# A hand-written order planned anew: transfers taken to land later, one quad more in the second chunk, other limits for the fillers

## The chip, the cores and the metric

The kernel runs on one core of a Trainium2 chip. The metric is device time in microseconds of one execution; several runs are made, and their median counts. One execution was also recorded by the hardware profiler; its span runs from the first to the last instruction of the program.

## What is computed

One transformer block with conditioning: a modulation vector from `c`, layer norm, attention with 32 heads of 20, a residual, a second layer norm, and a gated product of two projections, with a second residual. There are 2048 rows of 640, and 1536 hidden columns; all arrays are bf16.

```python
def _A_ref(x, wqkv, wo):
    qkv = (x @ wqkv).reshape(B, S, 3, H, Dh).transpose(2, 0, 3, 1, 4)
    q, k, v = qkv[0], qkv[1], qkv[2]
    scores = jnp.einsum('bhqd,bhkd->bhqk', q, k) * Dh ** (-0.5)
    p = _softmax(scores, axis=-1)
    o = jnp.einsum('bhqk,bhkd->bhqd', p, v)
    return o.transpose(0, 2, 1, 3).reshape(B, S, D) @ wo
def _B_ref(x, w_gate, w_up, w_down):
    h = jnp.einsum('bsd,df->bsf', x, w_gate) * jnp.einsum('bsd,df->bsf', x, w_up)
    return jnp.einsum('bsf,fd->bsd', h, w_down)
mod = (_silu(c) @ w_mod).reshape(c.shape[0], 6, 1, -1)
sa, ca, ga, sb, cb, gb = (mod[:, i] for i in range(6))
h = _layernorm(x) * (1 + ca) + sa
x = x + ga * _A_ref(h, A_wqkv, A_wo)
h = _layernorm(x) * (1 + cb) + sb
x = x + gb * _B_ref(h, B_w_gate, B_w_up, B_w_down)
```

## The kernel before

**A planner writes the order.** Nothing in this program is ordered by hand. While the program is built, `Sched` plays through all of the work with assumed durations, picks for each engine what to issue next, and `emit_program` then writes the five engines' instruction streams in exactly that order, with semaphore waits where one engine needs another's result. On the chip each engine keeps its order: where a result is later than the planner assumed, the engine waits, with all that stands behind. The assumed durations thus set the order and nothing else.

**Chunks, items, units.** The 2048 query rows are cut into seven chunks (`CHUNKS`: one of 512, six of 256). A chunk is worked through in eight items, each of four heads. An item's scores are cut into units: one head, and as many key tiles of 128 as fill 512 columns of a PSUM bank (four for a chunk of 512 rows, two for one of 256). The four heads of an item lie in four row groups of TensorE, so units of different heads run side by side (L1525).

**Two ways to exponentiate.** Most units go in pairs to ScalarE: one ACTIVATE of 128 x 1024 reads two banks and writes the ring `PP` (L1562). `QUADS` says how many quads (four units each) of each item of a chunk go to VectorE instead. For those VectorE adds a bias and rounds to int16 (L1586, one instruction a unit, into `DB`), masks the mantissa (L1618) and the exponent (L1626) of the whole quad into `DSS`, and a product completes the first of two terms: either one instruction on VectorE (L1623) or four pieces on GpSimd (L1638), whichever the planner finds free. The products with V (L2193) take one term from `PP`, but two from `DSS`.

**What TensorE interleaves.** Between two stretches of scores TensorE works on products with V, and on one round after another of other work: at the start layer norm transposes (L1128), the projections to K, Q (L1167, L1231) and V (L971 with wV), later the second half of the block for the chunk before ("suffix": output projection with `wo`, transposes, gate and up products with weights in `stg`, down products with `wd`). K and Q of most heads are laid out anew through DRAM: copied to `KPA` or `KPB`, written to `k_rows` or `q_rows` (L1277), and read back into `KT` (L1290) and `QT` (L1299). Finished attention goes through `OT`, `OTn`, `OcT` and then by DMA to `Ocp` (L1747). The weights in `stg` come through three buffers (L1932). All of these transfers stand in one queue, SyncE's, in the planner's order.

**What the planner assumes of transfers.** `Sched.finish_issue` (in the print below) sets `task.done`, the time at which a DMA is taken to have landed: issue, size over a rate, a latency, and for those issued after `DMA_M0` (60 us) a margin, `DMA_MARGIN`.

**Fillers.** The planner also models the clock of TensorE from the activity in windows of `HAM_W` ns (`roll`, with `HAM_MIN` as the least activity of a window that counts as busy). `do_fill` issues four matmuls that change no result, or a product that adds zero (`zero_fill`, L2524), where recent activity is below `FILL_HARD` or, for other picks, `FILL_MIN`; a full-width filler stands at L2552, one of four column groups at L2554.

**Stage settings.** `STAGE` maps an item's number (0 to 56, eight per chunk) to settings that hold from that item on: how many products with V are gathered before a switch (`PVMIN`, `PVMAX`, `PVCAP`), how long TensorE holds back for scores that are about to be ready (`HOLD`, `PVTOL`), when VectorE's units are pulled forward (`EAGER`, `D_LATE`, `D_RES`, `DL`), when a round's matmul is cut in two halves (`X_LATE`, `X_HALF`), and the limits above.

Of the kernel before, what the change touches and what calls it, by code (L numbers as in the profile page):

```python
# [26 lines left out]
DMA_SLOW = 0.0015  # L27
DMA_LAT = 1700.0
DMA_RATE_2 = 240.0
DMA_MARGIN = 500.0  # L30
DMA_M0 = 60000.0
STEAL_END = 66197.894
STEAL_GAP = 200
HAM_W = 3413.3
HAM_MIN = 3000.0
LKTOL = 300.0


# [92 lines left out]
class Sched:  # L131
# [78 lines left out]
    def roll(self, t):  # L210
        for i in range(4):
            w = int((t - i * HAM_W / 4) // HAM_W)
            while self.ham_w[i] < w:
                low = self.ham_act[i] < HAM_MIN
                if low:
# [18 lines left out]
    def finish_issue(self, task, start, dur):  # L234
        task.start = start
        if task.nbytes:
            early = self.t < DMA_EARLY
            b = max(self.dma_free, start + dur + (DMA_LAT_1 if early else 0.0))
            self.dma_free = b + task.nbytes / (DMA_RATE if early or task.firm else DMA_RATE_2)
            task.done = task.land or self.dma_free + (DMA_LAT_2 if early else DMA_LAT + DMA_SLOW * task.nbytes +  # L240
                                                      (0.0 if task.firm or start < DMA_M0 else DMA_MARGIN))
        else:
            task.done = start + dur + task.lat
        self.order[task.eng].append(task)
        self.all.append(task)
        self.left -= 1
        if task.on_start is not None:
            task.on_start(task)
        for u in task.users:
            u.nleft -= 1  # L250
            if u.nleft == 0:
                self._enable(u)
        task.users = []
# [99 lines left out]
def emit_program(nc, sched, nsem_dma=56):  # L353
# [121 lines left out]


CHUNKS = ((0, 512), (512, 256), (768, 256), (1024, 256), (1280, 256), (1536, 256), (1792, 256))
QUADS = ((0, 4, 3, 3, 3, 4, 4, 4), (1, 2, 1, 2, 2, 2, 1, 2), (2, 2, 1, 2, 2, 2, 1, 2), (2, 2, 1, 2, 2, 2, 1, 2), (2, 2, 1, 2, 2, 2, 1, 2), (2, 2, 1, 2, 2, 2, 1, 2), (2, 1, 2, 2, 2, 1, 2, 0))
SPLITJ = 1
QHALF = ((0, 0), (0, 0))  # L480
TB_GATE = 2
# [2 lines left out]
PV_KEEP = 2  # L484
# [10 lines left out]
EAGER = 7  # L495
# [3 lines left out]
XBACK = 0  # L499
HOLD = 110  # L500
PVTOL = 249
XDPRIO = 1.343
TPRIO = 0.75
# [19 lines left out]
D_LATE = 16  # L523
D_RES = 20
PVMIN, PVMAX, PVCAP = 2, 7, 12
# [13 lines left out]
GATE_F = (0.446, 0.5, 0.5, 0.5, 0.5, 0.5, 1.0)  # L539
FILL_MIN = 4190.746  # L540
HARD_FROM = 16000
FILL_HARD = 3500.0
FILL_T0, FILL_TH, FILL_MINH = 2300.0, 17000.0, 7500.0
FILL_MODE = 'P'
DUP_MIN = 0.0
# [17 lines left out]
NTERM = 2  # L563

STAGE = {
    0: {"XBACK": 0, "PVMAX": 14, "TPRIO": 0.75, "D_LATE": 16, "STEAL_GAP": 200, "EAGER": 9, "PVTOL": 249, "HOLD": 68.4, "PV_KEEP": 2, "X_HALF": 0.0, "XDPRIO": 1.343, "PVMIN": 2, "D_RES": 74, "LKTOL": 300.0, "X_LATE": -179.96, "FILL_MIN": 4190.746, "PVCAP": 12},
    2: {"DL": 0.376},
    4: {"PV_KEEP": 4, "XBACK": 1},
    5: {"EAGER": 5},
    6: {"STEAL_GAP": 303.6, "FILL_MIN": 4369.6},  # L570
    7: {"DL": 0.501, "EAGER": 12, "LKTOL": 214.2, "HOLD": 125.5},
    10: {"PVMAX": 5, "EAGER": 9, "FILL_MIN": 4030.1},
    11: {"DL": 0.443, "HOLD": 147.1, "PVCAP": 10, "EAGER": 1, "PVMAX": 13},
    12: {"DL": 0.459, "X_HALF": -78.2},
    13: {"DL": 0.417},
    14: {"X_HALF": 0.1, "D_RES": 9, "PVTOL": 152.2, "PVCAP": 7, "X_LATE": 15.9},
    15: {"PVTOL": 269.4, "X_LATE": 118.5},
    16: {"D_RES": 72, "HOLD": 109.5},
    17: {"XBACK": 1},
    18: {"HOLD": 26.4, "D_RES": 21, "PV_KEEP": 1, "FILL_MIN": 4542.4},  # L580
    19: {"DL": 0.471, "D_RES": 8, "EAGER": 5},
    20: {"DL": 0.391},
    21: {"EAGER": 9, "FILL_MIN": 4229.0, "PV_KEEP": 2},
    22: {"HOLD": 191.0},
    23: {"HOLD": 87.8, "PVMAX": 5},
    24: {"DL": 0.464, "STEAL_GAP": 189.1, "X_LATE": -52.5, "PVCAP": 14},
    25: {"DL": 0.549, "EAGER": 2, "PVMIN": 2, "PVMAX": 3, "STEAL_GAP": 204.7},
    26: {"DL": 0.411, "EAGER": 2, "PVMIN": 2, "PVCAP": 14},
    27: {"DL": 0.473, "X_LATE": -44.8},
    28: {"FILL_MIN": 4986.9},  # L590
    29: {"PVTOL": 317.6, "PVMAX": 4},
    30: {"EAGER": 11, "LKTOL": 263.3, "X_LATE": -102.4},
    31: {"FILL_MIN": 4003.8, "XBACK": 1, "PV_KEEP": 1},
    32: {"HOLD": 173.2, "X_HALF": 164.9, "PV_KEEP": 2},
    33: {"DL": 0.442, "PV_KEEP": 3, "LKTOL": 517.2},
    35: {"X_HALF": -49.0},
    36: {"DL": 0.524, "LKTOL": 130.0, "X_LATE": -54.5, "XBACK": 1},
    37: {"PVMAX": 9, "D_RES": 9, "X_LATE": 42.7, "D_LATE": 12},
    39: {"EAGER": 6, "X_LATE": -3.0, "XBACK": 2},
    40: {"FILL_MIN": 4681.4, "HOLD": 77.9},  # L600
    43: {"X_HALF": -36.2, "D_LATE": 18, "HOLD": 133.6, "STEAL_GAP": 190.9, "PV_KEEP": 2},
    44: {"PV_KEEP": 2, "X_HALF": -31.7},
    48: {"XBACK": 1},
    51: {"X_HALF": 18.4},
    56: {"D_RES": 25, "FILL_MIN": 4778.8},
}
XHALF = 1
STG_G0, STG_G, XC_G = 12, -10, -20
X_LATE = -24.052
X_HALF = 0.0  # L610
# [10 lines left out]
def build_kernel(nc, A_x, A_wqkv, A_wo, B_x, B_w_gate, B_w_up, B_w_down, c, w_mod, out):  # L621
# [710 lines left out]
    spans = [(0, CHUNKS[ci][1]) for ci, _ in items]  # L1332
    nqs = [QUADS[ci][j] for ci, j in items]
    if SPLITJ:
# [934 lines left out]
    def half_x(t):  # L2269
        cand = xcur[0]  # L2270
        if not XHALF or cand is None or id(cand) not in halves or ring() < RINGLOW:
            return False
        if any(d.done is None or d.done + SEM > t for d in cand.deps):
            return False
        sr = s_ready()
        if sr is None or t >= sr:
            return False
        start = mode_start(cand.mode, t)
        late = start + cand.dur - sr - X_LATE
        if late <= 0 or late - cand.dur / 2 > X_HALF:  # L2280
            return False
        first, cand.emits = halves.pop(id(cand))
        cand.dur /= 2
        h = Task("pe", cand.dur, first, cand.deps, ctr="pex", mode=cand.mode, name=cand.name, prio=cand.prio)
        h.seq = 0
        sc.left += 1
        sc.activity(start, h.dur * 2.37)
        sc.finish_issue(h, start, h.dur * clk())
        sc.pe_mode = h.mode
        sc.pe_end = start + h.dur * clk()  # L2290
        sc.free_at["pe"] = sc.pe_end
        nhalf[0] += 1
        return True
# [103 lines left out]
    def pick_pe(t):  # L2397
# [65 lines left out]
        if HOLD and sr is not None and t < sr <= t + HOLD and ring() >= RINGLOW:  # L2463
            return half_x(t)
        if sc.recent(t) < FILL_HARD and t > HARD_FROM and do_fill(t):
            return True
# [163 lines left out]
```

## Time and profile before

| what | value |
|---|---|
| runs | 810.54, 810.21, 807.32 us; median 810.21 |
| profiled execution: run time | 808.72 us |
| profiled execution: span | 806.9 us |
| mean granted TensorE clock | 0.998 |
| busy: PE / DVE / ACT / POOL | 790.6 / 691.5 / 765.1 / 395.4 us |
| instructions | 37691 |
| DMA | 64.65 MB, mean 80 GB/s |

How to read it: a matmul's end is modelled, and matmuls of different row or column groups overlap, so the busy time of PE says that it always had work in flight, not that it ran at its peak. Durations in a group are means of one instruction from start to end; where such instructions overlap in the pipeline, the step from one start to the next is shorter than the mean. Views that list instructions in order of time give the start in us from the beginning of the span, the length of the merged group, the engine, the line, what is written and read, the count, and in brackets how long the engine was idle before it and what ended that wait. Line numbers are those of the kernel before; in the changed kernel most lines stand one line earlier.

### The profile page before, as it was taken

Reading aid. Unit: us, or ns where it says so; the run is one execution under the profiler, and the core shown is the slowest. Engines: PE = TensorE matmul, PEld = TensorE weight load, DVE = VectorE, ACT = ScalarE, POOL = GpSimd, SP = SyncE. Lnnn points to the kernel's source line nnn. Section 1 sums busy time; section 2 is a strip of 40 time slices with the busy share of each in tenths; the row PEclk is TensorE's granted clock in tenths of the full one; section 3 lists DMA queues with packets and bytes.
Section 4 is the critical chain, followed back from the end, with each engine's and each line's share of the span. In section 5 each row is a group of like instructions: output and inputs, shape, how many; then the busy total and the mean of one; then the engine's idle time right before and its main releaser. Section 6 shows DMA issues by size and latency. Waiting matters only on the chain.

```text
span 806.9 us, 37691 instructions
## 1 busy us (share of the span) xinstructions
PE 790.6 (98%) x16551; PEld 377.7 (47%) x16551; DVE 691.5 (86%) x1392; ACT 765.1 (95%) x848; POOL 395.4 (49%) x408
## 2 busy tenths in 40 slices
PE   8999999999999999999999999999999999999998
PEld 3433433332244344444555555545554555455567
DVE  6979788889989999998798988999899989799654
ACT  6799899999999999999999999999999999999961
POOL 2345455556464564554636555543554455554300
PEclk9999999999999999999999999999999999999999
DMA  9743312212342441120052224312420244414420
GB/s 293 214 137 81 77 36 70 71 33 65 89 110 56 141 112 45 40 55 21 23 123 53 57 57 104 73 29 66 113 65 15 63 106 87 104 39 89 107 66 18
DMA packets 154313, 64.65 MB, mean 80 GB/s; under 512 B 116951, under 2 KB 154151, under 8 KB 154151
## 3 DMA queue, kind: packets, MB, share of 16 engines
q1 hardware_dynamic: 153223, 61.10, 29.8%
q8 instruction: 131, 2.15, 1.1%
q10 hardware_dynamic: 928, 1.15, 0.4%
q14 instruction: 31, 0.25, 0.1%
HBM read 50.63 MB, written 8.99 MB: 74 GB/s over the span
## 4 chain that ended last, share of the span: by engine, by line
PE 67%; ACT 20%; DVE 5%; issue 4%; DMA 3%; SPq 1%; POOL 0%; ACTq 0%; DVEq 0%
PE ps_all L1525 23%; ACT PP L1562 20%; PE ps_all L971 19%; PE ps_all L2193 16%; PE ps_all L1231 3%; PE ps_all L967 3%; DMA x<-in_A_x_dram 2%; DVE DB L1586 2%; DMA stg<-in_B_w_up_dram 1%; PE ps_all L1890 1%; DVE DSS L1618 1%; PE ps_all L1128 0%; DVE DSS L1626 0%; SPq L1747 0%; PE ps_all L2524 0%
## 5 line engine op out<-in xcount | busy, mean ns | idle before, releaser
L1562 ACT ACTIVATE PP<-ps_all 128x1024 bf16<-128x1024 f32 x812 | 749.5, 1108 | 8.0 <-PE ps_all L1525 4.0
L1638 POOL TENSOR_TENSOR DSS<-DB,DSS 128x512 bf16<-128x512 bf16 x280 | 317.3, 1155 | 290.7 <-DVE DSS L1626 255.1
L1586 DVE TENSOR_SCALAR DB<-ps_all 128x512 int16<-128x512 f32 x424 | 285.1, 683 | 49.8 <-PE ps_all L1525 46.4
L1525 PE MATMUL ps_all<-QT,KT 32*128 32x256 bf16 (+2 forms) x3648 | 319.9, 287 | 6.4 <-ACT PP L1562 2.5
L1525 PEld LDWEIGHTS ps_all<-QT,KT 32*128 32x128 bf16 x3648 | 93.2, 92 | 207.8 <-ACT PP L1562 149.3
L2193 PE MATMUL ps_all<-PP,Vf 128*32 128x256 bf16 (+2 forms) x2900 | 165.5, 291 | 0.8 <-DVE Vf L1320 0.7
L971 PE MATMUL ps_all<-h2T,stg 128*32 128x256 bf16 (+2 forms) x2728 | 124.8, 280 | 0.8 <-DMA stg<-in_B_w_up_dram 0.3
L2193 PEld LDWEIGHTS ps_all<-PP,Vf 128*32 128x32 bf16 (+1 forms) x2900 | 53.5, 94 | 79.3 <-issue 70.9
L2193 PE MATMUL ps_all<-DSS,Vf 128*32 128x256 bf16 (+1 forms) x1496 | 86.2, 290 | 0.0
L971 PEld LDWEIGHTS ps_all<-h2T,stg 128*32 128x32 bf16 x2728 | 61.8, 96 | 28.1 <-issue 21.0
L1626 DVE TENSOR_SCALAR DSS<-DB 128x2048 int16<-128x2048 int16 x106 | 74.0, 698 | 0.8 <-PE ps_all L2193 0.8
L1618 DVE TENSOR_SCALAR DSS<-DB 128x2048 int16<-128x2048 int16 x106 | 73.4, 693 | 0.5
L971 PE MATMUL ps_all<-wd,hprod 128*32 128x320 bf16 (+1 forms) x1364 | 62.4, 280 | 0.0
L1726 POOL TENSOR_TENSOR OTn<-OT,invT 128x256 bf16<-128x256 f32 (+1 forms) x49 | 34.6, 707 | 35.0 <-DVE invT L1724 34.9
L1623 DVE TENSOR_TENSOR DSS<-DB,DSS 128x2048 bf16<-128x2048 bf16 x36 | 44.9, 1248 | 0.1
L2193 PEld LDWEIGHTS ps_all<-DSS,Vf 128*32 128x32 bf16 x1496 | 34.5, 95 | 21.7 <-issue 14.6
L971 PE MATMUL ps_all<-wV,hT 128*32 128x160 bf16 x1280 | 38.7, 234 | 0.4 <-DVE DB L1586 0.2
L971 PEld LDWEIGHTS ps_all<-wd,hprod 128*32 128x32 bf16 x1364 | 30.9, 96 | 14.2 <-issue 11.2
L1718 DVE STREAM_TRANSPOSE OT<-ps_all 128x256 f32<-128x256 f32 (+2 forms) x57 | 27.1, 475 | 7.3 <-PE ps_all L2193 7.1
L1231 PE MATMUL ps_all<-hT,wk 128*32 128x512 bf16 (+1 forms) x360 | 32.8, 386 | 0.0
L971 PEld LDWEIGHTS ps_all<-wV,hT 128*32 128x32 bf16 x1280 | 24.4, 96 | 15.4 <-issue 8.2
L1231 PE MATMUL ps_all<-hT,wq 128*32 128x512 bf16 x375 | 31.5, 382 | 0.0
(133 smaller groups left out, 557.7 us busy)
## 6 DMA issues: line engine op xcount, KB each, us to landing
stg<-in_B_w_gate_dram SPq DMA_DIRECT2D x74, 160.0 KB
stg<-in_B_w_up_dram SPq DMA_DIRECT2D x74, 160.0 KB
KT<-k_rows SPq DMA_DIRECT2D x112, 32.0 KB
QT<-q_rows SPq DMA_DIRECT2D x48, 64.0 KB
Ocp<-OcT SPq DMA_DIRECT2D x164, 10.0 KB
wm<-in_w_mod_dram SPq DMA_DIRECT2D x3, 800.0 KB
x<-in_A_x_dram SPq DMA_DIRECT2D x7, 320.0 KB
k_rows<-KPA SPq DMA_DIRECT2D x16, 128.0 KB
```

What stands on the lines that cost most here:

```text
L971: return lambda e, b: e.matmul(ps[32 * x:32 * x + 32, b, c0 + o:c0 + o + w], lhs()[:, 32 * x:32 * x + 32], rhs() if w == n else rhs()[:, o ...
L1231: f = [lambda e, b_, k=k, x=x: e.matmul(ps[x:x + min(32, w - x), b_, :], wx[:, k, r0 + x:r0 + min(x + 32, w)], hT[tc][:, k, :], tile_posit ...
L1525: ems.append(lambda e, i=i, kt=kt: e.matmul(dstf()[:, i * u.n:(i + 1) * u.n], KT[32 * u.s:32 * u.s + 32, u.j, kt * 128:(kt + 1) * 128], QT ...
L1562: return e.activation(PPs[g % 2][:, cellp["p"], 0:nu * 512], ps[:, b0:b0 + nu, :].rearrange("p b c -> p (b c)"), AFT.Exp, scale=ESCALE)
L1586: return e.tensor_scalar(DBl[st_["slot"]][:, x * 512:(x + 1) * 512], bank(cell["b"]), EBIAS, 0.0, op0=ALU.add, op1=ALU.max)
L1618: return e.tensor_scalar(DSl[st_["ss"][0]][:, :], DBl[st_["slot"]][:, :], 0x7F, 0x3F00, op0=ALU.bitwise_and, op1=ALU.bitwise_or)
L1623: return e.tensor_tensor(d, DBl[st_["slot"]][:, :].bitcast(BF16), d, ALU.mult)
L1626: return e.tensor_scalar(DSl[st_["ss"][1]][:, :], DBl[st_["slot"]][:, :], 0x7F80, 2, op0=ALU.bitwise_and, op1=ALU.bitwise_or)
L1638: return e.tensor_tensor(d, DBl[st_["slot"]][:, x * w:x * w + w].bitcast(BF16), d, ALU.mult)
L1718: t1 = Task("dve", n * 1.1 + 70, lambda e: e.transpose(OT[:, 0:n], ps[:, item_info[it]["bank"], 0:n].rearrange("p (b q r) -> p b r q", q=3 ...
L1726: f3 = lambda e: e.tensor_tensor(OTn[:, 0:n].rearrange("p (b c r) -> p b r c", c=32, r=2), OT[:, 0:n].rearrange("p (b r c) -> p b r c", c= ...
L2193: ems.append(lambda e, i=i, kt=kt, stt=stt, stp=stp: e.matmul(ps[32 * s:32 * s + mc, bk, 0:u.n], Vf[:, (kt * H + 4 * u.j + s) * VW:(kt * H ...
```

## The change

The assumed landing of transfers is put later: `DMA_MARGIN` from 500 to 1000 ns for those issued after 60 us, and a new `EARLY_M` of 900 ns for those in the first 25 us whose priority number is 0.9 or more (the first half of the V weights, the third and fourth 512 rows of x, the second halves of the weights). `HAM_MIN` goes from 3000 to 3100 and `FILL_HARD` from 3500 to 3600. The first item of chunk 1 has two quads instead of one. `STAGE` is replaced in most of its entries. Since every one of these goes into the planner, the order of all five engines is another from the first microseconds on.

```diff
-DMA_MARGIN = 500.0
+DMA_MARGIN = 1000.0
+EARLY_M = 900.0
...
-HAM_MIN = 3000.0
+HAM_MIN = 3100.0
...
+            if early and not task.land and task.prio >= 0.9:
+                task.done += EARLY_M
...
-QUADS = ((0, 4, 3, 3, 3, 4, 4, 4), (1, 2, 1, 2, 2, 2, 1, 2), ...
+QUADS = ((0, 4, 3, 3, 3, 4, 4, 4), (2, 2, 1, 2, 2, 2, 1, 2), ...
...
-FILL_HARD = 3500.0
+FILL_HARD = 3600.0
...
 STAGE = {
-    0: {"XBACK": 0, "PVMAX": 14, "TPRIO": 0.75, "D_LATE": 16, "STEAL_GAP": 200, "EAGER": 9, "PVTOL": 249, "HOLD": 68.4, "PV_KEEP": 2, "X_HALF": 0.0, "XDPRIO": 1.343, "PVMIN": 2, "D_RES": 74, "LKTOL": 300.0, "X_LATE": -179.96, "FILL_MIN": 4190.746, "PVCAP": 12},
+    0: {"PVMIN": 2, "HOLD": 95, "PVTOL": 249, "D_RES": 58, "PVCAP": 6, "X_HALF": 0.0, "XDPRIO": 1.343, "FILL_MIN": 3463.3, "LKTOL": 300.0, "EAGER": 9, "PVMAX": 14, "X_LATE": -179.96, "TPRIO": 0.75, "STEAL_GAP": 200, "D_LATE": 16, "PV_KEEP": 2},
+    1: {"PVCAP": 15, "XBACK": 1, "FILL_MIN": 4629.7},
     2: {"DL": 0.376},
-    4: {"PV_KEEP": 4, "XBACK": 1},
-    5: {"EAGER": 5},
-    6: {"STEAL_GAP": 303.6, "FILL_MIN": 4369.6},
-    7: {"DL": 0.501, "EAGER": 12, "LKTOL": 214.2, "HOLD": 125.5},
+    4: {"HOLD": 58.0, "X_LATE": -39.3},
+    5: {"D_LATE": 7, "PVMAX": 3},
+    6: {"X_LATE": 168.4, "FILL_MIN": 5225.9, "HOLD": 156.4},
+    7: {"DL": 0.501},
...
```

What the two orders hold, counted: exponentials of ScalarE 812 and 810; first steps of VectorE 424 and 428; products on VectorE 36 and 40; pieces on GpSimd 280 and 268; matmuls 16,551 and 16,595; DMAs of SyncE the same. The stretches of scores on TensorE are 833 and 826.

More of the change, by code (lines that the diff above doesn't have):

```diff
@@ L477 @@
 CHUNKS = ((0, 512), (512, 256), (768, 256), (1024, 256), (1280, 256), (1536, 256), (1792, 256))
-QUADS = ((0, 4, 3, 3, 3, 4, 4, 4), (1, 2, 1, 2, 2, 2, 1, 2), (2, 2, 1, 2, 2, 2, 1, 2), (2, 2, 1, 2, 2, 2, 1, 2), (2, 2, 1, 2, 2, 2, 1, 2), (2, 2, 1, 2, 2, 2, 1, 2), (2, 1, 2, 2, 2, 1, 2, 0))
+QUADS = ((0, 4, 3, 3, 3, 4, 4, 4), (2, 2, 1, 2, 2, 2, 1, 2), (2, 2, 1, 2, 2, 2, 1, 2), (2, 2, 1, 2, 2, 2, 1, 2), (2, 2, 1, 2, 2, 2, 1, 2), (2, 2, 1, 2, 2, 2, 1, 2), (2, 1, 2, 2, 2, 1, 2, 0))
 SPLITJ = 1
@@ L567 @@
+    1: {"PVCAP": 15, "XBACK": 1, "FILL_MIN": 4629.7},
     2: {"DL": 0.376},
-    4: {"PV_KEEP": 4, "XBACK": 1},
-    5: {"EAGER": 5},
-    6: {"STEAL_GAP": 303.6, "FILL_MIN": 4369.6},
-    7: {"DL": 0.501, "EAGER": 12, "LKTOL": 214.2, "HOLD": 125.5},
-    10: {"PVMAX": 5, "EAGER": 9, "FILL_MIN": 4030.1},
-    11: {"DL": 0.443, "HOLD": 147.1, "PVCAP": 10, "EAGER": 1, "PVMAX": 13},
-    12: {"DL": 0.459, "X_HALF": -78.2},
-    13: {"DL": 0.417},
-    14: {"X_HALF": 0.1, "D_RES": 9, "PVTOL": 152.2, "PVCAP": 7, "X_LATE": 15.9},
@@ L577 @@
[L577 to L605, printed above, removed]
+    4: {"HOLD": 58.0, "X_LATE": -39.3},
+    5: {"D_LATE": 7, "PVMAX": 3},
+    6: {"X_LATE": 168.4, "FILL_MIN": 5225.9, "HOLD": 156.4},
+    7: {"DL": 0.501},
+    8: {"FILL_MIN": 2868.8},
@@ new lines @@
+    10: {"X_HALF": 69.3, "HOLD": 73.7, "PVMAX": 5},
+    11: {"DL": 0.443},
+    12: {"DL": 0.459, "HOLD": 108.3, "X_LATE": 6.6},
+    13: {"DL": 0.417},
+    15: {"X_LATE": 86.8},
+    16: {"HOLD": 135.0, "FILL_MIN": 4362.5},
+    17: {"X_LATE": -17.4, "LKTOL": 338.9, "HOLD": 52.0},
+    19: {"DL": 0.471, "PVMAX": 7, "HOLD": 113.6},
+    20: {"DL": 0.391, "PVMAX": 10},
+    21: {"X_LATE": -85.4, "PVMIN": 3},
+    24: {"DL": 0.464, "STEAL_GAP": 210.6, "X_LATE": -52.5, "PVCAP": 14, "HOLD": 116.4, "LKTOL": 98.1},
@@ new lines @@
+    25: {"DL": 0.549, "LKTOL": 370.4, "HOLD": 156.3},
+    26: {"DL": 0.411, "PVMIN": 1, "X_LATE": 2.0, "EAGER": 6, "X_HALF": 58.0},
+    27: {"DL": 0.473},
+    29: {"HOLD": 148.6, "D_LATE": 5, "LKTOL": 267.5, "D_RES": 36, "PVMAX": 3},
+    30: {"EAGER": 11},
+    31: {"X_LATE": -99.6, "HOLD": 173.2, "X_HALF": 164.9, "PV_KEEP": 2},
+    33: {"DL": 0.442, "PVMIN": 7, "PV_KEEP": 3, "X_HALF": 147.4},
+    34: {"PVMIN": 3, "X_HALF": 26.9, "STEAL_GAP": 91.8, "EAGER": 8, "X_LATE": 136.8, "D_RES": 25},
@@ L606 @@
+    35: {"X_HALF": 148.7},
+    36: {"DL": 0.524},
+    37: {"FILL_MIN": 4112.0, "EAGER": 8, "X_LATE": -201.5},
+    39: {"STEAL_GAP": 162.9, "EAGER": 9},
+    42: {"PVMAX": 8, "FILL_MIN": 4334.4, "PV_KEEP": 3},
+    43: {"HOLD": 127.6},
+    46: {"D_LATE": 20, "PV_KEEP": 3, "X_LATE": -80.9},
+    53: {"LKTOL": 820.1, "X_HALF": 73.5},
+    54: {"PVTOL": 279.6, "FILL_MIN": 4011.5, "X_HALF": 31.3},
 }
```

## The prediction

> **What bounds the kernel now.** I read the profiled execution: span 806.9 us, run time 808.72 us, so 1.8 us lie around the span; the median of the three runs (810.21) is 1.5 us above this run. First the chain that ended last and the costliest groups:
>
> ```profile
> PE 67%; ACT 20%; DVE 5%; issue 4%; DMA 3%; SPq 1%; POOL 0%; ACTq 0%; DVEq 0%
> ...
> L1562 ACT ACTIVATE PP<-ps_all 128x1024 bf16<-128x1024 f32 x812 | 749.5, 1108 | 8.0 <-PE ps_all L1525 4.0
> L1638 POOL TENSOR_TENSOR DSS<-DB,DSS 128x512 bf16<-128x512 bf16 x280 | 317.3, 1155 | 290.7 <-DVE DSS L1626 255.1
> L1586 DVE TENSOR_SCALAR DB<-ps_all 128x512 int16<-128x512 f32 x424 | 285.1, 683 | 49.8 <-PE ps_all L1525 46.4
> ...
> L1626 DVE TENSOR_SCALAR DSS<-DB 128x2048 int16<-128x2048 int16 x106 | 74.0, 698 | 0.8 <-PE ps_all L2193 0.8
> L1618 DVE TENSOR_SCALAR DSS<-DB 128x2048 int16<-128x2048 int16 x106 | 73.4, 693 | 0.5
> ...
> L1623 DVE TENSOR_TENSOR DSS<-DB,DSS 128x2048 bf16<-128x2048 bf16 x36 | 44.9, 1248 | 0.1
> ```
>
> Two engines share the bound: TensorE has most of the chain, but ScalarE's 812 exponentials form one almost unbroken stream. Second, ScalarE in order of time (start, length, count, idle before):
>
> ```profile
> 16.35 4.66 ACT L1562 ACTIVATE PP<-ps_all 128x1024 bf16<-128x1024 f32 x5
> ...
> 92.92 1.94 ACT L1562 ACTIVATE PP<-ps_all 128x1024 bf16<-128x1024 f32 x2 [2.77 <-PE ps_all L2193]
> ...
> 149.54 66.30 ACT L1562 ACTIVATE PP<-ps_all 128x1024 bf16<-128x1024 f32 x72
> ...
> 753.02 25.79 ACT L1562 ACTIVATE PP<-ps_all 128x1024 bf16<-128x1024 f32 x28 [0.58 <-PE ps_all L1525]
> ```
>
> The 72 exponentials from 149.54 come every (66.30 - 1.02)/71 = 0.92 us (1.02 is the length of a single one), although the group's mean length is 1.108: they overlap. So 0.92 is the price of one. The stream runs from 16.35 to 753.02 + 25.79 = 778.81; 812 x 0.92 = 747 of these 762.5 us is its own pace, some 15 us are stalls, and 28.1 us of tail follow. The time is start + count x pace + stalls + tail, and the change is costed in these terms.
>
> Third, the start, by stage (PE, weight loads, DVE, ACT, POOL busy, then granted clock):
>
> ```profile
> 17.50:20.00 2.50, 1.78 (x23) 0.51 (x18) 2.50 (x10) 2.50 (x4) 1.06 (x2) 1.00 0.70 179
> 20.00:22.50 2.50, 1.94 (x20) 0.97 (x20) 2.50 (x8) 1.91 (x3) 1.39 (x3) 0.89 1.11 332
> 22.50:25.00 2.50, 2.50 (x20) 1.17 (x22) 2.23 (x7) 1.83 (x3) 0.37 (x2) 0.50 0.31 65
> 25.00:27.50 2.50, 2.50 (x61) 1.32 (x56) 1.89 (x7) 1.04 (x3) 2.12 (x5) 0.92 0.83 296
> ```
>
> TensorE idles at 17.5 to 22.5, then its clock falls to half while it is full. Fourth, the instructions before which TensorE (and once VectorE) stood still, in order of time:
>
> ```profile
> 17.48 0.49 DVE L1072 BATCH_NORM_STATS2 st<-x 128x6 f32<-128x320 bf16 x1 [0.86 <-DMA x<-in_A_x_dram]
> ...
> 20.56 0.68 PE L1128 MATMUL ps_all<-ident,xn 128*128 128x128 bf16 x9 [0.94 <-DVE xn L1046]
> ...
> 92.49 0.40 PE L2193 MATMUL ps_all<-PP,Vf 128*32 128x512 bf16 x3 [0.70 <-DVE Vf L1320]
> ...
> 232.89 0.40 PE L1525 MATMUL ps_all<-QT,KT 32*128 32x256 bf16 x6 [1.01 <-DVE KPB L1243]
> ...
> 412.09 0.46 PE L971 MATMUL ps_all<-h2T,stg 128*32 128x256 bf16 x12 [0.26 <-DMA stg<-in_B_w_up_dram]
> ...
> 752.20 0.46 PE L971 MATMUL ps_all<-h2Tt,stg 128*32 128x256 bf16 x12 [0.80 <-DMA stg<-in_B_w_up_dram]
> ```
>
> **The change part by part.** The two programs' instruction orders, compared engine by engine, give counts; the rows above give prices.
>
> (1) One more quad in chunk 1 takes four units from ScalarE: 812 exponentials become 810, 2 x 0.92 = **-1.8 us**, as ScalarE's other work stays (one more moved evacuation, 0.37 us, against all else alike).
>
> (2) The same quad on VectorE: 4 x 0.683 (L1586) + 0.693 + 0.698 = 4.1 us; and multiplications on VectorE rise from 36 to 40 while GpSimd's pieces fall from 280 to 268 (the new quad's included): 4 x 1.248 = 5.0 us more VectorE, 12 x 1.155 = 13.9 us less GpSimd. VectorE is idle for 807 - 691.5 = 115 us in all and 7.6 of the 95 us from 210 to 305, where the 4.1 fall. Cover: that idle time, most of it spent waiting for scores (46.4 us before L1586). Without cover, up to 9.1 us. I take **+0.5**, near the covered end, since VectorE mostly waits for TensorE and not the reverse. TensorE gets 16 more products from DSS and 8 fewer from PP: 8 of 256 columns, 0.2 us (eight take 0.23 from start to start around 231.2), within the same 0.5.
>
> (3) Fewer passes of scores. TensorE's order has 826 separate stretches of scores instead of 833; two are the lost exponentials, five are separate passes for VectorE's units that now ride along. A stretch costs 0.33 us to the next other work plus some 0.1 to come back (228.19 to 228.52, for example): 5 x 0.43 = 2.15 us of TensorE. Where ScalarE's pace sets the end this buys nothing, where TensorE does, all of it. Half: **-1.1** (0 to -2.15).
>
> (4) The start. ScalarE's and GpSimd's orders are the same there. VectorE's differs: the two small sd operations for the second 512 rows stood behind the BATCH_NORM_STATS2 that waited for a landing until 17.48; now they stand ahead of it. GpSimd's two powers (0.55 each) then end near 17.8 instead of 19.4, and the last two xn (19.71 to 20.51) come near 18.4 to 19.1, as only one statistic and three V copies stand ahead. TensorE's 0.94 us wait for xn shrinks or goes. One filler (four 512-column matmuls, 0.22 us) is put in at 15.9, ahead of the V products; it lies in idle time, since TensorE waits later anyway. Five fillers that stood near 78 us are gone, also from idle time; the zero-adding fillers stay about as many. With TensorE busier in 18.5 to 22, the half clock may not come: it cost (0.11 + 0.50 + 0.08) x 2.5 = 1.7 us of a full TensorE. At most 0.94 + 1.7 = 2.65; at least 0, because VectorE is full from 30 to 35 and could give the gain back. I take **-2.0**, as from 22.5 to 37.5 TensorE is full in every row.
>
> [...]
>
> (5) Transfers taken to land later. No DMA is added (709 SP instructions in both); the planner asks for what a transfer brings later, and the 354 waits of TensorE for DMAs remain. What can go are the stalls seen: 0.80 (752), 0.26 (412) and 1.01 (232, via q_rows<-KPB, for whose landing VectorE's KPB copy waited with six q_rows pieces in the SP queue): 2.07 us. Behind the one at 752 stood five Ocp<-OcT issues, 4.30 us on SP, ahead of the weights; the new SP order still has such groups of five ahead of stg, so I count on later use, not on earlier issue. Bounds 0 and -2.07; I take **-1.5**. On SP, KT<-k_rows and k_rows<-KPA are mixed more finely between 30 and 90 us; their 0.43 us issues move by one to three places, hidden at nothing; if a score waits for one, it costs 0.43 to 1.3, inside the next term.
>
> (6) Bursts. Where other work between two stretches of scores exceeds 0.92 - 0.43 = 0.49 us, exponentials are late. At 0.22 us per four 512-column matmuls, 0.137 for 320 and 0.07 for 160, the old burst at 90 us is 2.34 us and, with a 1.03 wait, gave the 2.77 idle of ScalarE; the new order has 1.58 there (and lighter neighbours, 0.48 instead of 0.88): about -2.6. But it has new ones: 1.55 and 1.24 at the 48th and 49th stretch (beside the column products of w_mod), 1.37 and 0.95 at the 375th and 376th, beyond the budget by 1.06 + 0.75 + 0.88 + 0.46 = 3.2. Net **+0.6**; bounds -2.6 (all new ones absorbed by the rings of PP) and +3.2 (the old stall stays as a wait).
>
> (7) Tail: the same instructions after the last score (24.8 us of matmuls by the same prices, 24.9 now): **0**, bounds +-0.5.
>
> Sum: -1.8 + 0.5 - 1.1 - 2.0 - 1.5 + 0.6 = -5.3; span 801.6, run 803.4, against the median 810.2 - 5.3 = **804.9**.
>
> **Rivals.** (a) *The gain is swallowed*: a new order brings as many new late arrivals as it removes, and the two exponentials remain: 810.2 - 1.8 = 808.4. For it: the stalls above are single events, each by chance of the order. Against: the 0.94 and 0.86 waits have a visible cause that the new order moves.
>
> (b) *The clock falls anyway.* A low window elsewhere before 25 us halves the clock again: 1.7 of part 4 is lost, about 806.6. [...] For it: still two stretches in 17 to 21 with two matmuls of scores and little else. Against: the long idle is shorter.
>
> (c) *VectorE becomes the bound* (slower than before): in chunk 1 and where multiplications came to it, its 9.1 us do not fit into idle time because TensorE, in strict order, then waits for L1586's banks and DSS. Price 9.1 instead of 0.5: 804.9 + 8.6 = 813.5. It decides against the kernel once over 5.8 of the 9.1 us lie on the path. For it: VectorE 92% busy from 210 to 305, and TensorE's waits for VectorE rise from 808 to 827. Against: 7.6 us idle there, and GpSimd eased by 13.9.
>
> **How the numbers follow.** Forecast 0.50, own range 801 to 808.5; (a) 0.20; (b) 0.14; (c) 0.16. Together the range is 800 to 813: the bounds' best sum (-11) and worst (+7 and more) need every term at its end. 0.5% is 4.05 us, about what a measurement can tell from no change: faster means under 806.2. Three quarters of the forecast (0.37), just under half of (b) (0.06) and 0.03 of (a): 0.46. Slower (over 814.3): under half of (c) and tails, 0.12. Same: 0.42.
>
> **What would show it.** Part 1: 810 exponentials at 0.92. Part 4: no row at clock 0.50 and the first 20 exponentials done 2 us sooner. Part 5: no stall over 0.5 us before L971 with stg. Part 6: no idle over 1.5 us before L1562 near 90 us; new ones near 70 and 365 us. I am wrong if VectorE's idle in 210 to 305 goes towards zero with waits for L1586 growing, or if the stream, not the start, is where time is lost.

## The result, and the profile after

| | before | after |
|---|---|---|
| median (range, runs) | 810.08 (807.32 to 810.67, 8) | 804.93 (803.65 to 807.38, 8) |
| profiled execution: run time, span | 808.72, 806.9 | 805.59, 803.8 |
| first exponential, last exponential, last one to the end | 16.35, 777.79, 29.1 | 16.35, 774.69, 29.1 |

The changed kernel takes 5.15 us less by the medians. The ratio, estimated from all of the runs, is 0.9951 with an interval of 0.993 to 0.9973; the ratio of the two medians, 0.9936, lies within it. (One of the 12 runs of the kernel of paragraph 6 below fell into a slow state, 1106.68 us at a mean clock of 0.557, and is left out of its ratio.) Its chain of waits and its groups, in the order in which those of before were shown (lines stand one lower):

```profile
PE 77%; ACT 14%; DVE 5%; issue 2%; DMA 1%; SPq 1%; POOL 0%; DVEq 0%; ACTq 0%
...
L1561 ACT ACTIVATE PP<-ps_all 128x1024 bf16<-128x1024 f32 x810 | 748.5, 1090 | 6.7 <-PE ps_all L1524 4.8
L1637 POOL TENSOR_TENSOR DSS<-DB,DSS 128x512 bf16<-128x512 bf16 x268 | 305.0, 1157 | 290.6 <-DVE DSS L1625 254.2
L1585 DVE TENSOR_SCALAR DB<-ps_all 128x512 int16<-128x512 f32 x428 | 285.5, 681 | 50.5 <-PE ps_all L1524 48.0
...
L1622 DVE TENSOR_TENSOR DSS<-DB,DSS 128x2048 bf16<-128x2048 bf16 x40 | 51.5, 1287 | 0.0
```

ScalarE's share of the chain falls from 20% to 14%, and its idle time before exponentials from 8.0 to 6.7 us. VectorE's extra quad shows as 428 first steps and 40 products, GpSimd's relief as 268 pieces. ScalarE in order of time:

```profile
36.60 18.44 ACT L1561 ACTIVATE PP<-ps_all 128x1024 bf16<-128x1024 f32 x20 [0.75 <-PE ps_all L1524]
...
91.26 2.86 ACT L1561 ACTIVATE PP<-ps_all 128x1024 bf16<-128x1024 f32 x3 [1.16 <-PE ps_all L2192]
...
374.56 262.18 ACT L1561 ACTIVATE PP<-ps_all 128x1024 bf16<-128x1024 f32 x284 [0.36 <-PE ps_all L1524]
637.04 138.83 ACT L1561 ACTIVATE PP<-ps_all 128x1024 bf16<-128x1024 f32 x151 [0.29 <-PE ps_all L1524]
```

The 284 from 374.56 come every (262.18 - 1.02)/283 = 0.92 us, as before. The group of 28 that began behind a weight load (753 us before) is gone: the last group runs through. At 91 us 1.16 us of idle stand where 2.77 stood.

The matmul that waited longest for a transfer in this execution, and the stages of the start (PE, weight loads, DVE, ACT, POOL busy, then granted clock):

```profile
94.31 0.40 PE L1524 MATMUL ps_all<-QT,KT 32*128 32x512 bf16 x4 [0.82 <-DMA QT<-q_rows]
```
```profile
17.50:20.00 2.50, 2.35 (x37) 1.05 (x37) 2.31 (x8) 2.50 (x3) 1.09 (x2) 1.00 0.88 214
20.00:22.50 2.50, 2.50 (x31) 1.27 (x29) 2.50 (x7) 2.50 (x4) 0.79 (x2) 1.00 0.99 292
22.50:25.00 2.50, 2.50 (x50) 1.20 (x52) 2.50 (x9) 1.94 (x3) 0.93 (x3) 1.00 0.32 44
```

No half clock at the start (there is one behind the wait at 94 us, from 96.86 on), and the group of 20 exponentials begins at 36.60 where the profile of before had 38.59. That looks as if the prediction's step on the start had come true with its 2.0 us. The experiments say otherwise.

For the readings below I take each start of an exponential less the one before it, and call what exceeds 0.905 us (the shortest regular step) *lateness*; summed over a stretch it says what that stretch cost the stream.

### The profile page after: what moved, and what is told of

Same layout as the page of the kernel before. It is cut to its first block, busy times and chain, and to the rows that moved or that the text cites. A ratio compares the mean times of both kernels' runs of the same rounds, so it can differ in the third digit from the quotient of the medians.

```text
span 803.8 us, 37761 instructions
## 1 busy us (share of the span) xinstructions
PE 790.4 (98%) x16595; PEld 380.6 (47%) x16595; DVE 697.8 (87%) x1401; ACT 764.8 (95%) x847; POOL 386.0 (48%) x396
## 4 chain that ended last, share of the span: by engine, by line
PE 77%; ACT 14%; DVE 5%; issue 2%; DMA 1%; SPq 1%; POOL 0%; DVEq 0%; ACTq 0%
PE ps_all L1524 26%; PE ps_all L970 21%; PE ps_all L2192 19%; ACT PP L1561 14%; PE ps_all L1230 4%; PE ps_all L966 3%; DVE DB L1585 2%; PE ps_all L1889 1%; PE ps_all L1166 1%; PE ps_all L1127 1%; DVE DSS L1617 1%; PE ps_all L2523 0%; DVE DSS L1625 0%; DMA QT<-q_rows 0%; PE ps_all L991 0%
## 5 line engine op out<-in xcount | busy, mean ns | idle before, releaser
L1637 POOL TENSOR_TENSOR DSS<-DB,DSS 128x512 bf16<-128x512 bf16 x268 | 305.0, 1157 | 290.6 <-DVE DSS L1625 254.2
L1585 DVE TENSOR_SCALAR DB<-ps_all 128x512 int16<-128x512 f32 x428 | 285.5, 681 | 50.5 <-PE ps_all L1524 48.0
L2192 PE MATMUL ps_all<-PP,Vf 128*32 128x256 bf16 (+2 forms) x2892 | 163.6, 291 | 0.5 <-DVE KPB L1242 0.3
L970 PE MATMUL ps_all<-h2T,stg 128*32 128x256 bf16 (+2 forms) x2716 | 122.9, 281 | 0.3 <-DVE DB L1585 0.2
L2192 PE MATMUL ps_all<-DSS,Vf 128*32 128x256 bf16 (+1 forms) x1512 | 88.7, 291 | 0.0
L1617 DVE TENSOR_SCALAR DSS<-DB 128x2048 int16<-128x2048 int16 x107 | 77.2, 722 | 0.8
L1625 DVE TENSOR_SCALAR DSS<-DB 128x2048 int16<-128x2048 int16 x107 | 73.2, 684 | 0.8 <-PE ps_all L2192 0.8
L1622 DVE TENSOR_TENSOR DSS<-DB,DSS 128x2048 bf16<-128x2048 bf16 x40 | 51.5, 1287 | 0.0
L2192 PEld LDWEIGHTS ps_all<-DSS,Vf 128*32 128x32 bf16 x1512 | 36.5, 95 | 20.9 <-issue 12.4
L1230 PE MATMUL ps_all<-hT,wk 128*32 128x512 bf16 x360 | 32.3, 382 | 0.0
```

The lines of the kernel that those rows point to most:

```text
L970: return lambda e, b: e.matmul(ps[32 * x:32 * x + 32, b, c0 + o:c0 + o + w], lhs()[:, 32 * x:32 * x + 32], rhs() if w == n else rhs()[:, o ...
L1230: f = [lambda e, b_, k=k, x=x: e.matmul(ps[x:x + min(32, w - x), b_, :], wx[:, k, r0 + x:r0 + min(x + 32, w)], hT[tc][:, k, :], tile_posit ...
L1585: return e.tensor_scalar(DBl[st_["slot"]][:, x * 512:(x + 1) * 512], bank(cell["b"]), EBIAS, 0.0, op0=ALU.add, op1=ALU.max)
L1617: return e.tensor_scalar(DSl[st_["ss"][0]][:, :], DBl[st_["slot"]][:, :], 0x7F, 0x3F00, op0=ALU.bitwise_and, op1=ALU.bitwise_or)
L1622: return e.tensor_tensor(d, DBl[st_["slot"]][:, :].bitcast(BF16), d, ALU.mult)
L1625: return e.tensor_scalar(DSl[st_["ss"][1]][:, :], DBl[st_["slot"]][:, :], 0x7F80, 2, op0=ALU.bitwise_and, op1=ALU.bitwise_or)
```

## The experiments

Where the order is edited, the planner has finished and its list of tasks is altered behind it, so that everything else stays in place: `move_ahead(tasks, mark)` puts tasks ahead of another in their engines' orders, `move_behind` behind it. Each timed kernel ran beside before on the same chip; before's medians there were 808.5 to 809.8. After itself was timed only once, in the section above, so where a later kernel is set against its 804.93, the two were not timed side by side.

### 1. Both kernels looked at once more

> The kernel before, unchanged, profiled once more. If the stalls of TensorE that the prediction counted on belong to the order, the waits near 20.6, 92.5, 232.9 and 752.2 us are there again within 0.3 us of their length, and the clock falls to half once between 18 and 26 us. If they were chance events of one execution (the rival), at least two of the four are missing or lie elsewhere.

> The changed kernel, unchanged, profiled once more. Expected from the order: full clock from 5 to 28 us, no wait of TensorE for xn over 0.4 us, the group of 20 exponentials starting near 36.6 us, and the wait for a QT transfer near 94 us again. The half clock that one profile shows near 97 us is expected to be a chance event: of eight runs two have a mean clock below 1.000, so it is absent with 3 chances in 4. The rival says it belongs to the order and comes again.

808.40 and 804.01 us. In this execution of before nothing is slow at the start: the group of 20 exponentials begins at 36.39 us, and the clock is full:

```profile
20.00:22.50 2.50, 2.50 (x32) 1.26 (x33) 2.50 (x7) 2.50 (x4) 1.04 (x3) 1.00 1.00 298
22.50:25.00 2.50, 2.50 (x58) 1.31 (x60) 2.50 (x10) 1.99 (x3) 1.56 (x4) 1.00 0.46 125
```

The late landing of x, the wait for xn and the half clock, on which the prediction built its largest term, belonged to one execution. Of the other three waits that the expectation names, those for Vf and for the weights at 752 us came again (0.70 and 0.92 us), and the one near 232 us came twice as long (2.11). What differs between these two executions lies elsewhere (lateness in us, by number of the exponential):

| | to 20 | 20 to 60 | 60 to 100 | from 100 | last begins at |
|---|---|---|---|---|---|
| before, repeated | 5.55 | 0.79 | 4.86 | 15.99 | 777.51 |
| after, repeated | 5.54 | 1.42 | 2.55 | 15.03 | 773.12 |

With the two exponentials fewer, 2 x 0.905 = 1.81, these sums make up the 4.4 us between the last exponentials. From 100 on, before has three single late ones of 2.12 (at 232 us), 0.88 (412) and 1.03 (753). The first and the last stand behind transfers; the profile puts TensorE's wait at 412 down to VectorE's copy into OcT, but it goes when the weights are issued earlier (paragraph 3). After has 0.45 and 0.73 near 222 and 232, and new ones of 0.32 to 0.47 at its 307th, 376th, 459th and 660th exponential. The wait for QT at 94 us, which was expected again, is not there in the repeat of after, nor is the half clock behind it: its lateness from the 60th to the 100th exponential is 2.55, that of the first execution 4.83.

### 2. The start, from both sides

In before (`sd`, powers and `xn` of the second 512 rows go ahead of the statistics `st8` of the third), and in after the other way round, behind and among the copies `vs` into Vf:

```diff
+    move_ahead([q_sd2, q_sd3], q_st8[0])
+    move_ahead([q_pw2, q_pw3, q_xn2, q_xn3], q_st8[1])
```
```diff
+    move_behind([q_sd2, q_pw2], vs[0])
+    move_behind([q_sd3, q_pw3], vs[1])
+    move_ahead([q_st8[0]], vs[0])
+    move_ahead(dv[k:k + 2], vs[3])
```

> The order before on every engine, but on VectorE the two sd operations, and the two last xn, of the second 512 rows stand ahead of the batch norm statistics of the third (as in the changed order); no filler is added. Theory (part 4 of the prediction): TensorE gets xn 1 to 1.4 us sooner, its 0.94 us wait goes, the half clock probably with it, and the stream of exponentials stays 1.5 to 2.0 us ahead to the end: about 808.2 against 810.1. Rival: VectorE, full from 30 to 35 us, gives it back: 810 within 0.4, with the group of 20 exponentials still starting at 38.6.

> The changed order on every engine, but VectorE's start (sd, xn, statistics, V copies of the second 512 rows) stands as it did before; the filler stays. Theory: the wait for xn returns with about 0.9 us or more, the group of 20 exponentials starts near 38.5 instead of 36.6, and the time rises by 1.5 to 2.0 us to about 806.7. Rival (the filler alone holds the clock and the wait was covered): less than 0.7 us.

Before with the new start: 808.89 against 809.77, ratio 0.9986 (0.9968 to 1.0004). After with the old start: 805.31, ratio to before 0.9951 (0.993 to 0.9973), the same as after's own. These intervals are 3 to 3.5 us wide and would leave room for 2 us; the profiles decide. The group of 20 in the first and in the second, in a view up to 45 us:

```profile
36.89 8.36 ACT L1562 ACTIVATE PP<-ps_all 128x1024 bf16<-128x1024 f32 x9 [0.68 <-PE ps_all L1525]
```
```profile
36.52 9.27 ACT L1561 ACTIVATE PP<-ps_all 128x1024 bf16<-128x1024 f32 x10 [0.75 <-PE ps_all L1524]
```

It begins no sooner with the new start than with the old one. Nor is this two executions alone: of the seven profiles with the old start, one has 7.77 us of lateness up to the 20th exponential (the first of before) and six have 5.55 to 5.90; the six with the new start have 5.51 to 6.11. So the order at the start moves the stream by nothing that could be seen here, and the prediction's -2.0 falls. Whether the new start makes a half clock rarer stays open: 7 of the 12 runs with it had a mean clock of 1.0, against 5 of the 19 of before beside them, but so had 7 of the 8 of after with the old start.

### 3. Weights issued earlier (412 and 752 us)

`sp` is SyncE's queue as a list; 676 and 409 are the first loads of the two pairs.

```diff
+    move_ahead(sp[676:678], sp[672])
+    move_ahead(sp[409:411], sp[407])
```

> The order of before, with two changes in SyncE's queue alone: the pair of weight loads into stg that is issued near 747 us is moved ahead of four of the five Ocp<-OcT issues that stood before it, and the pair near 407 us ahead of the last Ocp<-OcT and of the one load behind it. Theory (transfers decide, part 5 of the prediction, with issue earlier in place of use later): TensorE's waits before L971 with stg at 412 us (0.72 in the repeat of before) and at 752 us (0.92) go, and with them 0.88 + 1.03 us of late exponentials; the median falls by 1 to 1.9 us, to about 808.5. Rival (swallowed): the waits go, but the stream of exponentials is late elsewhere, since the Ocp copies land 0.9 to 3.4 us later; change 0 to -0.5. Third: the waits stay, because the buffers and not the queue were late; no change.

808.04 against 809.0, ratio 0.9992 (0.9967 to 1.0017). Both waits for stg are gone from its profile, and so are the two late exponentials; but the median's gain of 1.0 is not clear of nothing. One likely reason is the clock: two of these 12 runs had a mean clock of 1.0, against 11 of the 29 of before beside them. The same profile shows a half clock, at the third transfer. By stage, this kernel:

```profile
229.50:232.00 2.50, 0.87 (x22) 0.38 (x15) 1.15 (x3) 1.16 (x2) 2.13 (x2) 0.98 0.30 93
232.00:234.50 2.50, 2.50 (x37) 1.05 (x38) 1.84 (x4) 1.59 (x2) 0.00 (x0) 0.50 0.85 200
234.50:237.00 2.50, 2.50 (x58) 1.15 (x50) 2.13 (x6) 1.85 (x3) 2.08 (x2) 0.84 0.49 121
```

and before, repeated, in the first two of these stages:

```profile
229.50:232.00 2.50, 0.39 (x15) 0.10 (x6) 0.91 (x2) 0.87 (x1) 1.78 (x2) 1.00 0.31 91
232.00:234.50 2.50, 2.50 (x63) 1.28 (x63) 2.50 (x7) 2.15 (x3) 0.20 (x1) 1.00 0.84 201
```

TensorE stands still in the first stage of both (1.63 us here, 2.11 in the repeat). Behind it, here, the clock is at half for 3.41 us: 37 matmuls in place of 63 in 2.5 us, and two exponentials late by 0.85 and 0.76, 1.61 in sum. In the repeat the longer wait was followed by the full clock. So a late transfer can have a second price that is paid in some executions; in the profiles of paragraphs 4 and 6, which have such a stretch too, it is 1.46 and 0.96 us.

### 4. The burst at 90 us

`v51` are the five steps of the V product and `cast` its copy into Vf, `gab2` and `gab5` those of w_mod, `pv` the three products with V, `s73` the stretch of scores behind them.

```diff
+    move_ahead(v51, gab2[-5])
+    move_ahead(cast[:1], gcast[0])
+    move_ahead(pv, gab5[0])
+    move_ahead([s73], rest)
```

> The order of before with one place altered, near 87 to 92 us. TensorE: the five steps of one V product (wV, 160 columns) go ahead of five of w_mod's, the three products with V that free the ring PP go ahead of the second half of w_mod (two blocks of 20), and the stretch of scores behind them goes ahead of 40 matmuls with wV. VectorE: the copy into Vf that these products need goes ahead of one copy into gab and of the 1.29 us multiplication of wo, behind which it stood. Theory (the burst of part 6 was a wait of ScalarE for a slot of PP, behind a wait of TensorE for Vf, behind VectorE's multiplication): the 2.77 us of idle of ScalarE at 90.7 us shrinks to about 1, the exponentials from the 60th to the 100th lose some 2.5 us in place of 4.86, and the median falls by 1.5 to 2.5 us, to about 808. Rival (swallowed): the burst goes, but later exponentials are late instead; 0 to -0.5. Rival (the amount of work in the burst, not the wait, makes the idle): the idle stays above 2 us.

808.48 against 809.0, ratio 0.9993 (0.9969 to 1.0017). ScalarE in order of time:

```profile
89.25 1.94 ACT L1562 ACTIVATE PP<-ps_all 128x1024 bf16<-128x1024 f32 x2 [1.21 <-PE ps_all L2193]
92.42 2.93 ACT L1562 ACTIVATE PP<-ps_all 128x1024 bf16<-128x1024 f32 x3 [1.24 <-PE ps_all L2193]
```

The idle of 2.77 is now two of 1.2; the lateness from the 60th to the 100th exponential falls from 4.86 to 4.37 only. The wait for Vf behind VectorE's multiplication was real, but with it moved the stream is late at the next place. That fits the rival, by which the amount of other work in that stretch makes most of the idle; no run took work out of it.

### 5. The stores into q_rows

In before's queue, as the repeat shows it (SyncE):

```profile
224.66 2.99 SPq L1299 DMA_DIRECT2D QT<-q_rows  x4
227.69 3.33 SPq L1277 DMA_DIRECT2D q_rows<-KPB  x6
```

what VectorE did, and behind it TensorE:

```profile
231.09 0.69 DVE L1243 TENSOR_SCALAR KPB<-ps_all 128x512 bf16<-128x512 f32 x1 [1.97 <-DMA q_rows<-KPB]
```
```profile
231.93 0.40 PE L1525 MATMUL ps_all<-QT,KT 32*128 32x256 bf16 x6 [2.11 <-DVE KPB L1243]
```

Six stores stand behind four loads of QT that the plan first uses at 404 us or later; VectorE's next copy into KPB waits for the stores to land, VectorE's queue with it, and TensorE for VectorE. The edit puts the loads behind the stores (its second line; the first does the same with two loads and two stores a little earlier in the queue):

```diff
+    move_behind(sp[245:247], sp[248])
+    move_behind(sp[253:257], sp[262])
```

> The order of before with one stretch of SyncE's queue altered, near 215 to 231 us: six QT<-q_rows loads, first used after 390 us, are put behind eight q_rows<-KPB stores that the planner had put behind them, and whose landing VectorE's next copy into KPB waits for. Theory (one late transfer decides, with the clock): the wait before KPB at 231 us (1.5 to 2.0 us on VectorE, 1.6 to 2.4 on TensorE in the profiles of before's order) goes, and with it the 3.4 us at half clock that two of the four profiles of this order show right behind it; the excess of the exponentials there (2.1 to 4.1 us) falls to under 0.7, the median falls by 2.5 to 3.5 us to about 806, and most runs (over 60% in place of a third) have a mean clock of 1.0. Rival (swallowed): the wait goes but the exponentials are late elsewhere; 0 to -0.7. [...]

806.13 against 808.87, ratio 0.9974 (0.9946 to 1.0002). The queue, the copy, and ScalarE of this kernel:

```profile
223.93 3.46 SPq L1277 DMA_DIRECT2D q_rows<-KPB  x6
227.44 1.77 SPq L1299 DMA_DIRECT2D QT<-q_rows  x4
```
```profile
228.93 0.68 DVE L1243 TENSOR_SCALAR KPB<-ps_all 128x512 bf16<-128x512 f32 x1
```
```profile
92.94 466.94 ACT L1562 ACTIVATE PP<-ps_all 128x1024 bf16<-128x1024 f32 x505 [0.23 <-PE ps_all L2193]
560.05 189.00 ACT L1562 ACTIVATE PP<-ps_all 128x1024 bf16<-128x1024 f32 x206 [0.17 <-PE ps_all L1525]
```

The copy into KPB waits for nothing, and 505 exponentials run through where the stream of before broke at 232 us. Of its 12 runs, 9 had a mean clock of 1.0; of the 27 of before on the same chip, 12 had. The interval just reaches no change, so the size is not shown by this run alone; that the wait at this place is gone is plain in the profile.

### 6. The three together

The edits of paragraphs 3, 4 and 5 in one kernel.

> The order of before with three places altered together: the stores into q_rows near 215 to 231 us (as in the run that alters these alone), the two pairs of loads into stg near 407 and 747 us, and the burst at 87 to 92 us. Theory (the gain of the change is the sum of such single late arrivals): -3 for the stores, -0.7 for stg and -0.7 for the burst, the middles of what was measured or is expected of each alone, so -4.4 of the 809 to 810 us of before: about 805, as low as after, though with 812 exponentials and the old quads and stretches. Rival (after owes its time to fewer exponentials and stretches): not under 807.

804.28 against 808.87, ratio 0.9954 (0.9931 to 0.9977). With before's 812 exponentials, quads and stretches it is as fast as after within the intervals, as the theory said, and the rival (not under 807) is out. The three alone gave -1.0, -0.5 and -2.7, -4.2 in sum; together -4.6. Its profiled execution has a new wait of the same kind, TensorE, and SyncE's queue ahead of it:

```profile
442.51 0.72 PE L971 MATMUL ps_all<-h2T,stg 128*32 128x256 bf16 x12 [1.87 <-DMA stg<-in_B_w_up_dram]
```
```profile
432.41 4.67 SPq L1747 DMA_DIRECT2D Ocp<-OcT  x5
```

Five issues of 4.67 us ahead of the weights, and the half clock from 442.50 to 445.91 behind the wait: it fell into this execution (805.8 us of span, 807.6 of run time), while ten other runs of it had a mean clock of 1.0 and took 803.75 to 805.57 us.

### 7. The price of an engine's time

```diff
+            ts.emits = ts.emits * 2
```
```diff
+        act_of[g].emits = [lambda e, b0=b0: e.activation(
+            junk[:, :], ps[:, b0, 0:384], AFT.Exp, scale=ESCALE)] + act_of[g].emits
```

> The order of after with 60 of the score stretches between the 150th and the 750th issued twice (the same matmuls to the same banks, 0.22 us of TensorE each, 13 us in all): added work of TensorE, nothing else. Part 3 of the prediction priced TensorE's time at a half: +6.5 us. Rival (ScalarE's pace alone sets the end): 0 to +2. Rival (TensorE is the bound): +11 to +13.

> The order of after with 50 additional exponentials of 128 x 384 on ScalarE, one ahead of every twelfth of those from the 150th to the 750th, written to a tile that nobody reads (about 0.37 us each, 18.5 us in all): added work of ScalarE, nothing else. If ScalarE's pace sets the end, as parts 1 and 3 of the prediction have it, +16 to +18.5. If TensorE and ScalarE share it by halves, +9. If TensorE is the bound, 0 to +4.

812.71 and 818.34 us, against after's 804.93: +7.8 for 13.0 us of TensorE (a price of 0.60), +13.4 for 50 x 0.372 = 18.6 us of ScalarE (0.72; 0.372 is the step that one such exponential adds to the stream). As after was not timed beside them, the prices are rough. Neither engine alone is the bound; each us on either costs more than half of itself. In the ScalarE run each of the 50 steps is late by 0.37 or more, and the small latenesses elsewhere (under 0.3 us, from the 100th exponential on) shrink from 12.2 to 8.1 us: where ScalarE is later, TensorE has more time to be ready. Both lie between the expectation by halves and that of a single bound; the half of the prediction was a little low.

### 8. After with its own late places altered

> The order of after with its own late places altered. SyncE: the stores q_rows<-KPB near 215 to 228 us go ahead of the loads QT<-q_rows that are first used after 370 us. TensorE near 89 us: one V product goes ahead of three steps of w_mod's, and three products with V that free PP go ahead of the next V product; VectorE: the copy into Vf goes ahead of one copy into gab and one multiplication of wo. Theory (late single arrivals decide): the two waits for KPB (0.45 and 0.73 of late exponentials at 221 and 231 us) go, the 1.16 us idle of ScalarE at 91 us falls under 0.4; 0.9 to 1.9 us less than after's 804.9, about 803.5. Rival (swallowed, as after is paced by TensorE and ScalarE together): 804.5 to 805.

```diff
+    move_ahead([sp[244], sp[247], sp[248]], sp[241])
+    move_ahead([sp[259]], sp[251])
+    move_ahead(sp[260:263], sp[257])
+    move_ahead(v61, gab5[0])
+    move_ahead(cast[:1], gcast[0])
+    move_ahead(pv, v71[0])
```

803.71 us (802.76 to 805.04, 10 runs, all with a mean clock of 1.0), ratio to before 0.9946 (0.9927 to 0.9965). The two waits for KPB are gone (lateness from 100 on 13.92 in place of 15.03); the idle at 91 us again only moved (2.66 in place of 2.55 from the 60th to the 100th). It is faster than before; against after, which was not timed beside it, 1.2 us lie within what the two intervals leave open.

### 9. The settings of transfers alone, planned anew

```diff
-DMA_MARGIN = 500.0
+DMA_MARGIN = 1000.0
+EARLY_M = 900.0
```

> Before planned anew with the two settings of transfers alone (margin 1000 in place of 500, 900 for the early ones); quads, fillers' limits and stage settings as before. The plan is another one throughout: 812 exponentials, 807 stretches of scores in place of 833, and 32.0 us of TensorE's work behind the last stretch in place of 24.8. Theory (the settings only pick another plan, and a plan is worth its single late arrivals and its tail): +7.2 for the tail, -2 to -3.5 for the late stores into q_rows, which here may or may not come: 812 to 816, with the time from the last exponential to the end at 36 us in place of 29.1. Rival (later landings are themselves the gain): 804 to 807. Rival (fewer stretches pay at TensorE's measured price of 0.6 for each us: 26 x 0.43 x 0.6 = -6.7): 806 to 810.

823.64 against 808.52, ratio 1.0187 (1.0147 to 1.0228): 15 us slower, more than any theory had. From the last exponential to the end it takes 36.7 us in place of 29.1, as the +7.2 said. The other half is in the stream, whose last exponential begins at 785.3 (777.5 in the repeat of before), though there are 26 stretches fewer and the place near 232 us costs only 0.58. Its largest loss is no transfer; TensorE, GpSimd and ScalarE:

```profile
529.02 2.48 PE L974 MATMUL ps_all<-h2T,stg 128*32 128x256 bf16 x80 [0.20 <-DVE DB L1589]
531.81 0.41 PE L2196 MATMUL ps_all<-DSS,Vf 128*32 128x256 bf16 x8 [0.31 <-POOL DSS L1641]
```
```profile
530.60 1.16 POOL L1641 TENSOR_TENSOR DSS<-DB,DSS 128x512 bf16<-128x512 bf16 x1 [2.20 <-DVE xn L1855]
```
```profile
532.49 2.85 ACT L1565 ACTIVATE PP<-ps_all 128x1024 bf16<-128x1024 f32 x3 [4.46 <-PE ps_all L2196]
```

The plan puts 80 gate and up products ahead of the products with V that free PP; those then wait 0.31 us more for a piece of DSS that GpSimd began late, behind 2.20 us of waiting that the profile puts down to VectorE's xn, and ScalarE is idle for 4.46 us. So later landings are not a gain by themselves: they pick another plan, and this one is bad.

## Why the prediction was right, and where not

The forecast (804.9) met the median (804.93), and in part by luck: the start (-2.0) and the stretches (-1.1) did not come, while transfers and bursts together brought some 2.5 us more than their terms.

**(1) Two exponentials fewer, -1.8**: the count and the 0.92 came. By the price of 0.72 measured for ScalarE's time they are worth 1.3.

**(2) The quad on VectorE, +0.5**: right. From 210 to 305 us VectorE is busy for 87.31 us in the repeat of after and 86.17 in that of before, and one wait of TensorE for L1585 (0.59 us at 308) makes an exponential 0.32 late. Rival (c), 9.1 us on the path, did not come.

**(3) Five stretches fewer, -1.1**: not to be seen. By the price of 0.60 it should be -1.3, but the small latenesses (under 0.3 us, from the 100th on) sum to 12.30 in the repeat of after and 11.95 in that of before: what left the stretches came back between them. That before with three places mended is as fast as after, at 812 exponentials and 833 stretches, fits this but does not show it alone, as after has late places of its own.

**(4) The start, -2.0**: the step that failed. It took 0.86 us of late landing, 0.94 of wait and 1.7 of half clock from one execution and put them down to the order. The repeat of before has none of them, and with the swap undone in after, or done alone in before, the stream begins no sooner or later for it. What the prediction named as its sign of being wrong, that the stream and not the start is where time is lost, is what the runs show.

**(5) Transfers, -1.5, at most -2.07**: that these waits belong to the order was right, the size was not, and the way in which they go was another. The prediction counted on later use, not on earlier issue. In the repeat of after, SyncE's queue itself differs at both places: the weights stand ahead of the five Ocp issues (a pair at 741.38 us, the five from 745.65), and the stores behind two loads of QT (from 224.72) in place of four. The three waits cost 2.12 + 0.88 + 1.03 of lateness in the repeat, of which after's kept 1.18: -2.85, beyond the bound. In the first execution of each the same places sum to 2.37 and 0.44, -1.93, inside it: the size depends on the execution. Mending these places in before gave 2.7 (the stores) and 1.0 (the weights) by the medians, neither clear by itself. The 1.01 us read for the stores was the shortest of five: the profiles of before's order have 1.01, 2.11, 1.96, 1.63 and 2.38 us there.

**(6) Bursts, +0.6**: in the two repeats -2.3 near 90 us, +0.6 from the 20th to the 60th exponential and +1.2 at the 376th, 459th and 660th: -0.5 in sum, within its bounds. The -2.6 that the prediction sets for the old burst is more than the figures beside it give (2.34 + 1.03 - 1.58 + 0.88 - 0.48 = 2.19).

**(7) The tail, 0**: 29.1 us in both.

**Rival (b), the clock,** was looked for at the wrong place. That a low window by itself halves the clock was the prediction's assumption: behind waits of 2.11 and 1.96 us at 232 us (before repeated, and with the new start) it stayed at 1.0. Of the 82 runs of before that stood beside the experiments, 32 had a mean clock of 1.0 and a mean time of 806.9; 31 had 0.998 (what one stretch of 3.41 us at half takes off: 3.41 x 0.5/806 = 0.002) and 809.8; 19 had less. Of after's 8, 6 had 1.0, at a mean of 804.6. So at the full clock the two orders lie 2.3 us apart, and the rest of the gain goes with the clock, which the new order seldom loses: the four kernels made from after by edits kept it in 30 of 32 runs.

What costs the old order its clock seems to be in the main the wait for the stores into q_rows. Before and the three kernels made from it that keep this wait (paragraphs 2, 3 and 4) had a mean clock of 1.0 in 46 of 118 runs; the two without it (5 and 6) in 19 of 24. Compared at a mean clock of 1.0 alone, before with the stores mended has a mean of 805.8 against 806.7 on the same chip, and with all three places 804.4. So of the 2.7 us of the stores about 0.9 come at the full clock, and the rest goes with the rarer half clock. These runs do not say whether a wait alone, without the half clock, is also longer in such executions.

What stays open: which of the settings made the plan of after a good one. Planning anew with the settings of transfers alone gave another plan throughout, so the settings can't be told apart in that way, and no others were tried alone.

## What to carry to other kernels

A stall in one profiled execution is a sample. Before pricing it, look at a second execution of the same kernel, and at the clock and time of every run: what comes in each profile belongs to the order, what comes once need not.

Where a queue carries transfers with very different times of need, look for those that free a buffer behind those that are used much later. Six loads put back by a few places in one queue brought, by the medians, about half of what the whole new plan did (2.7 of 5.15).

With a planner, a setting's direction says little of the result; compare the plans' late places and their tails.

## What the runs showed of the hardware

The clock fell to half behind waits that sum to less than the stretch at half clock that followed. All five stretches at half clock that the profiles show within the work last 3.41 us, at a granted clock of 0.50 (before, 21.97 to 25.38 us; after, 96.86 to 100.27), and in the 3.41 us ahead of each TensorE stood idle for 1.14 (before, 21.97 us), 1.06 (after, 96.86), 1.63 and 2.33 (before's order altered, 231.9) and 1.86 (442.5). The amount alone does not decide: waits of 2.11 and 1.96 at the same place (before repeated, and with the new start) were followed by none. What does decide, no run here shows.
